# Retention and gated MLP on one core: the first pair's residual as matmuls, tiles claimed at evacuation, and a new written-out order

## The chip, the cores and the metric

The kernel runs on one core of one Trainium2 chip, with the other cores idle. The metric is device microseconds of one launch; times are medians of several runs, and a difference of about 1% is what a measurement of this kernel can tell from none. The core's engines are PE (TensorE, whose weight loads are shown apart as PEld), DVE (VectorE), ACT (ScalarE), POOL (GpSimd) and SP (SyncE, which here only issues DMAs). Each takes its own instructions in order; semaphores tie them together.

## The reference

```python
scores = scale * np.matmul(q, k.transpose(0, 1, 3, 2))
Dmat = np.where(rel >= 0, gamma[:, None, None] ** rel[None, :, :], 0.0)
ret = scores * Dmat[None, :, :, :]
x = np.matmul(ret, v)                      # 8 batches, 8 heads, 576 rows, 64 wide
...                                        # heads side by side: x is (8, 576, 512)
h = gelu(x @ w_in)                         # 512 -> 1024
u, v = h[..., :512], h[..., 512:]
v_n = (v - mu) / np.sqrt(var + 1e-06) * g_ln
v_s = np.einsum('ts,bsd->btd', w_sg, v_n) + b_sg[None, :, None]
out = x + (u * v_s) @ w_out
```

Inputs and output are float32. The output's last sum, `x +`, is the residual that the title speaks of.

## The kernel before, in words

**Tiling.** Two batches make a pair; there are 4 pairs. A pair has 2 x 576 = 1152 rows, which are 9 tiles of 128 rows; the middle tile holds the last 64 rows of both batches. The retention goes by blocks: 4 blocks of 256 rows and one block for the middle tile, 5 to a pair, 20 in all.

**Retention, per block.** q is scaled by a power of gamma, k is cast, v is scaled by the inverse power (`a_prep`, lines 391 to 405, any of ACT, DVE and POOL). q and k are transposed on PE against an identity (`a_T`, 441 for whole 128x128 tiles, 451 for 64x64 ones) and copied out of PSUM (`a_Tev`, lines 254 on ACT and 255 on DVE). PE makes the scores (`a_S`, 524), DVE multiplies them by a mask into the tile `ret` (`a_Sev`, 537 and 540). PE makes the state products k-times-v (`a_Z`, 560), whose sums over blocks DVE makes (`a_Zsum`, 585 and 588), with a bf16 copy `zb`. PE adds `ret` times v and q times state (`a_O`, 606), and ACT or DVE copy the result into `xT`, which holds x transposed (`a_Oev`, 254 and 255).

**MLP, per tile.** PE makes the v half of `x @ w_in` (`m_V`, 680), ACT its gelu into the tile `vg` (687), DVE its mean and variance (695, 696), POOL the inverse root (`m_rs`, 700 to 703), ACT or DVE the normalised `vn` (`m_norm`, 712, 714). PE makes the u half, two tiles at a time (`m_U`, 736), ACT its gelu into `uT` (747). Per batch and column group PE makes the row mixing `w_sg @ v_n` (`m_W`, 757), two PSUM tiles each, and DVE multiplies them into `uT` (767). Then, per tile, PE makes `uT @ w_out` (`m_O`, 789), and DVE adds the residual and writes the float32 tile `ob` (`m_Oev`, 806), which a DMA stores (818, or 815 twice for a middle tile).

**The residual before.** x stands transposed in `xT`. A DMA transpose on SP's queue (`m_X`, 798) brings each tile back as `xr`, and DVE adds it. The constant `XP` is the number of leading pairs that go another way: for those, four matmuls against an identity per tile add x inside PSUM (lines 782 to 787), and ACT copies the sum out (804). Before, `XP` is 0.

**What sets the order.** All work is a list of some 900 jobs. The table `ORDER` gives their order by number; a letter behind a number names the engine where several can do it (D for DVE, A for ACT, G for POOL, F for a transpose of whole tiles), and `fN` puts N filler matmuls of 128 columns on constants (`warm`) ahead of the next PSUM tile that is taken. The costs and due times written at the jobs have no effect once the table is given; only the order, the letters and the buffers count.

**Buffers.** PSUM has two pools: `pp`, 2 tiles, for transposes, scores and `a_O`; and `d`, 4 tiles, for everything else. SBUF tiles are taken in turn: `ob` 4, `xr` 5, `vg` 3, `ld` (float32 loads) 8, `ldq` 2.

**Start.** SP loads q, k, v of the first two blocks, then the next q (1 MB), the v half of `w_in` (1 MB, into `xT`'s space), further k and v, then the u half of `w_in` (1 MB, into `uT`'s space). PE's first instruction waits for three small DMAs into `rsrc` (824); DVE then works on the columns (`col_math`, 832 to 840), which give the correction rows `row4b` (851).

## Time and profile before

| what | value |
| --- | --- |
| median of 3 runs | 209.96 us (208.62 to 210.59) |
| the profiled execution's own time | 209.28 us |
| its span, first to last instruction | 207.6 us |
| around the span | 1.68 us |
| DVE, ACT, POOL busy | 79%, 56%, 54% of the span |
| queue q1 (all of SP's DMAs) | 49.28 MB, 95.5% of 16 engines' span |
| DMA transposes of `xT` into `xr` | 36, median 3.9 us from issue to landing |
| stores of 128 x 512 | 31, median 3.6 us to landing |

The profile gives busy time by engine, the chain of work that ended last, groups of instructions by line, and a timeline. A line of the timeline reads: start, duration, engine, line, operation, tile written and tiles read, shape, count, and in brackets how long the engine sat idle before it and who ended that. In the chain, "issue" is time in which the engine waited for nothing that the profile shows. The span is what the engines did; the time of a run is that plus the 1.68 us around it.

### The profile page before, as it was taken

The page shows a single profiled execution, that of the slowest core. Times are in us where ns is not written, and L with a number is a line of the kernel's source. Part 1 is how long each engine was busy: PE and PEld are TensorE (multiplying, and loading weights), DVE is VectorE, ACT ScalarE, POOL GpSimd, SP SyncE. Part 2 cuts the span into 40 slices and gives each one's busy share as a digit, 9 for nine tenths or more (in the row PEclk, how much of TensorE's full clock was granted, in tenths as well). Part 3 has the DMA queues.
Part 4 walks back from the last instruction along what each step waited for, and adds up shares of the span by engine and source line. Part 5 has one row for each costly group of instructions (what it writes and reads, how often), then busy time and mean ns, then how long its engine had stood idle before and what let it go on. Part 6 is the DMA issues. An engine that isn't in the chain of part 4 may idle for free.

```text
span 207.6 us, 7418 instructions
## 1 busy us (share of the span) xinstructions
PE 184.6 (89%) x3132; PEld 128.5 (62%) x3163; DVE 163.5 (79%) x313; ACT 115.6 (56%) x184; POOL 112.2 (54%) x163
## 2 busy tenths in 40 slices
PE   0684979989999999999999999997999999999980
PEld 0563646668777676666767866665577666575740
DVE  3879979569989887797989975999776985866661
ACT  5326677799948648797845654450838328233000
POOL 8687566978953356674959399375462220202000
PEclk9999999999999999999999999999999999999998
DMA  5999999999999999999999999899998946372656
GB/s 173 346 384 342 289 219 279 356 335 380 228 228 194 296 280 225 232 323 342 188 314 220 221 281 192 227 256 238 191 225 178 139 126 202 75 226 80 183 176 202
DMA packets 91029, 49.77 MB, mean 240 GB/s; under 512 B 42027, under 2 KB 84339, under 8 KB 90995
## 3 DMA queue, kind: packets, MB, share of 16 engines
q1 hardware_dynamic: 90976, 49.28, 95.5%
q8 instruction: 25, 0.41, 0.9%
q14 instruction: 10, 0.07, 0.1%
q10 hardware_dynamic: 18, 0.00, 0.0%
HBM read 32.94 MB, written 9.44 MB: 204 GB/s over the span
## 4 chain that ended last, share of the span: by engine, by line
PE 78%; issue 2%; DMA 2%; DVE 1%; ACT 0%; DVEq 0%; SPq 0%
PE wp L757 19%; PE hu L736 15%; PE hv L680 14%; PE op L789 13%; PE pp L606 7%; PE pp L524 3%; PE pp L441 3%; PE zp L560 2%; DMA xr<-xT 2%; PE pp L451 1%; PE wtp L878 1%; DVE ob L806 1%; ACT vg L687 0%; DVE xT L255 0%; DVE run L588 0%
## 5 line engine op out<-in xcount | busy, mean ns | idle before, releaser
L537 DVE TENSOR_TENSOR ret<-pp,msk 128x1024 bf16<-128x1024 f32 x32 | 38.4, 1213 | 3.1 <-PE pp L524 1.6
L405 POOL TENSOR_TENSOR vb<-ld,gpow 128x1024 bf16<-128x1024 f32 (+1 forms) x19 | 33.4, 1767 | 13.3 <-DMA ld<-in_v_dram 8.2
L757 PE MATMUL wp<-wT,vn 128*128 128x288 bf16 x256 | 36.8, 286 | 1.3 <-DVE run L588 1.3
L736 PE MATMUL hu<-xT,w_in 128*128 128x256 bf16 (+1 forms) x320 | 36.6, 262 | 0.5 <-DVE w_in L255 0.5
L680 PE MATMUL hv<-w_in,xT 128*128 128x512 bf16 x126 | 34.4, 379 | 2.7 <-ACT xT L254 1.4
L789 PE MATMUL op<-w_out,uT 128*128 128x512 bf16 (+1 forms) x135 | 34.2, 373 | 0.7
L767 DVE TENSOR_TENSOR uT<-wp,uT 128x288 bf16<-128x288 f32 x64 | 26.5, 448 | 9.6 <-PE wp L757 9.3
L736 PEld LDWEIGHTS <-w_in 128*128 128x128 bf16 x320 | 28.0, 98 | 7.7 <-DVE w_in L255 0.7
L687 ACT ACTIVATE vg<-hv 128x512 f32<-128x512 f32 x36 | 21.4, 595 | 18.2 <-PE hv L680 15.5
L254 ACT ACTIVATE xT<-pp 128x512 bf16<-128x512 f32 (+1 forms) x34 | 17.1, 551 | 24.0 <-PE pp L606 20.6
L700 POOL TENSOR_SCALAR mv<-mv 128x2 f32<-128x2 f32 (+1 forms) x20 | 5.1, 255 | 46.1 <-DVE mv L696 45.7
L806 DVE TENSOR_TENSOR ob<-op,xr 128x512 f32<-128x512 f32 (+1 forms) x37 | 24.5, 672 | 7.0 <-PE op L789 4.4
L757 PEld LDWEIGHTS <-vn 128*128 128x128 bf16 x256 | 24.2, 98 | 9.3 <-issue 1.5
L695 DVE BATCH_NORM_STATS2 bst<-vg 128x6 f32<-128x512 f32 x36 | 24.6, 684 | 5.3 <-ACT vg L687 5.3
L405 POOL TENSOR_TENSOR qb<-ldq,gpow 128x1024 bf16<-128x1024 f32 x13 | 25.6, 1980 | 0.7 <-DMA ldq<-in_q_dram 0.7
L712 ACT ACTIVATE vn<-vg,mv 128x512 bf16<-128x512 f32 x27 | 21.6, 810 | 7.1 <-POOL mv L703 7.0
L747 ACT ACTIVATE uT<-hu 128x512 bf16<-128x512 f32 x36 | 20.7, 594 | 7.8 <-PE hu L736 7.5
L680 PEld LDWEIGHTS <-xT 128*128 128x128 bf16 x144 | 13.5, 98 | 13.8 <-ACT xT L254 1.8
L789 PEld LDWEIGHTS <-uT 128*128 128x128 bf16 x148 | 13.7, 98 | 13.3
L701 POOL TENSOR_TENSOR mv<-mv,mhalf 128x2 f32<-128x2 f32 (+1 forms) x20 | 13.8, 690 | 1.7
L254 ACT ACTIVATE qT<-pp 128x2048 bf16<-128x2048 bf16 (+1 forms) x6 | 10.4, 1734 | 7.5 <-PE pp L441 7.5
L757 PE MATMUL wp<-wT,vmid 128*128 128x288 bf16 x64 | 13.1, 286 | 0.0
(113 smaller groups left out, 250.4 us busy)
## 6 DMA issues: line engine op xcount, KB each, us to landing
ld<-in_k_dram SPq DMA_DIRECT2D x16, 512.0 KB, 5.5
ld<-in_v_dram SPq DMA_DIRECT2D x16, 512.0 KB, 6.0
out_dram<-ob SPq DMA_DIRECT2D x31, 256.0 KB, 3.6
ldq<-in_q_dram SPq DMA_DIRECT2D x7, 1024.0 KB, 7.2
out_dram<-ob SPq DMA_DIRECT2D x10, 128.0 KB, 2.4
xT<-in_moe_w_sg_dram SPq DMA_DIRECT2D x2, 576.0 KB, 7.0
ld<-in_q_dram SPq DMA_DIRECT2D x2, 512.0 KB, 4.8
xT<-in_moe_w_in_dram SPq DMA_DIRECT2D x1, 1024.0 KB
```

The costliest lines, as they stand in the source:

```text
L254: return nc.scalar.activation(dst, src, Act.Copy)
L405: ve.tensor_tensor(dst, src, g.unsqueeze(len(src.shape) - 1).to_broadcast(list(src.shape)), op=Alu.mult)
L537: ins = nc.vector.tensor_tensor(ret[:].rearrange("p r (k t) -> p (r k) t", k=2), sc[:].rearrange("p r (k t) -> p (r k) t", k=2), (msk2 if ...
L680: ins = nc.tensor.matmul(hv[:], xTs[p][:, m, kk, :], w_in[:, kk, F2:], start=(kk == 0), stop=(kk == KK - 1))
L687: unfence(nc.scalar.activation(vgs[i][:], cur.pop(("hv", i))[:], Act.Gelu_apprx_tanh), ("V", i))
L695: nc.vector.bn_stats(bst[:], vgs[i][:])
L712: nc.scalar.activation(dst, vg[r, :], Act.Identity, scale=mv[r, s, 2:3], bias=mv[r, s, 3:4])
L736: ins = nc.tensor.matmul(hu[:, n, :], w_in[:, kk, 128 * c:128 * c + 128], xTs[p][:, m:m + w, kk, :], start=(kk == 0), stop=(kk == KK - 1), ...
L757: ins = nc.tensor.matmul(ps[half][:], vns[NT * p + tile_of(e, j)][e][:, 128 * c:128 * c + 128], wT[e][j][:, lo:lo + HS], start=(j == 0), s ...
L767: ins = nc.vector.tensor_tensor(uTs[p][:, c, col:col + HS], cur.pop(("wp", b, c, half))[:], uTs[p][:, c, col:col + HS], op=Alu.mult)
L789: ins = nc.tensor.matmul(op[:], uTs[p][:, c, r], w_out[:, c, cs], start=(p >= XP and c == 0), stop=(c == KK - 1), skip_group_check=True)
L806: ins = nc.vector.tensor_tensor(ob[:, cs], op[:], cur["xr", i][:].rearrange("p j r -> p (j r)")[:, cs], op=Alu.add)
```

## The change

`XP` becomes 1: the nine tiles of the first pair get x by four matmuls each against the identity, and ACT writes their `ob`; nine DMA transposes go. The tiles `ret`, `vg` and `ob` are taken by the job that writes them and no longer by the matmul ahead of it. `vg` has 4 tiles (3), `mv` 4 (3), `vn` 13 (11). The stores of the last pair may go on ACT's queue. The scaling of v of the first block and of q of the second are put behind the column arithmetic in the planner's dependencies. `ORDER` is new, with more fillers: `f15 f24` ahead of PE's first instruction, `f11` later.

```diff
-    XP = 0
+    XP = 1
...
-BUFS = dict(... vg=3, mv=3, vn=11, ob=4, xr=5, pp=2, d=4)
+BUFS = dict(... vg=4, mv=4, vn=13, ob=4, xr=5, pp=2, d=4)
...
     def a_S(b, g):
-        st[b, "ret", g] = new("ret", [128, 2, 512], BF)
     def a_Sev(b, g):
-        ret = st[b, "ret", g]
+        ret = st[b, "ret", g] = new("ret", [128, 2, 512], BF)
...
     def m_V(i):
-        vgs[i] = new("vg", [128, F2], F32)
     def m_Vg(i):
+        vgs[i] = new("vg", [128, F2], F32)
...
     def m_O(i, hf=None):
-        if not hf:
-            cur["ob", i] = new("ob", [128, DM], F32)
     def m_Oev(i, hf=None):
+        if ("ob", i) not in cur:
+            cur["ob", i] = new("ob", [128, DM], F32)
...
-    def m_store(i, hf=None):
+    def m_store(i, hf=None, eng="SP"):
+        dma = nc.sync if eng == "SP" else nc.scalar
...
-                               deps=[J["ld", b, "q"]] + jqs, ...
+                               deps=[J["ld", b, "q"]] + ([j_cm] if b == 1 else []), behind=jqs[0] if c else None, ...
-        jvv = add("POOL", ..., deps=[J["ld", b, "v"]], ...
+        jvv = add("POOL", ..., deps=[J["ld", b, "v"]] + ([j_cm] if not b else []), ...
...
-    "2 3 8 4 97 9 75 98D 0 100F 10 1 78 14 102D 101A 81 79 ...
+    "2 f15 3 4 f24 8 97 9 75 98 0 10 1 100F 78 14 74 99 101 5 ...
```

In the program this removes 16 of the 64-wide transposes and adds 8 of 128 (all counted as matmuls), adds 36 residual matmuls with their weight loads and 9 filler instructions, moves 9 `ob` from DVE to ACT, and moves copies of transposed tiles from ACT to DVE (ACT loses four of 128x2048 into `qT` and one into `kT`; DVE gains the same). POOL gives five scalings of v and q to DVE and takes one. On SP the nine transposes of the first pair go and six store instructions move to ACT. In the first loads, v of the first block goes ahead of q of the second, and the u half of `w_in` goes ahead of v of the third block.

**Place 1: PE, end of the first pair's middle block.** The last state products of the retention are followed by the v half's products before:

```order
L606 LDWEIGHTS zb
L606 MATMUL pp<-qT,zb 64x128
L606 LDWEIGHTS zb
L606 MATMUL pp<-qT,zb 64x128
L680 LDWEIGHTS xT
L680 MATMUL hv<-w_in,xT 128x512
L680 LDWEIGHTS xT
L680 MATMUL hv<-w_in,xT 128x512
```

and now by eight products of the u half:

```order
L605 LDWEIGHTS zb
L605 MATMUL pp<-qT,zb 64x128
L605 LDWEIGHTS zb
L605 MATMUL pp<-qT,zb 64x128
L735 LDWEIGHTS w_in
L735 MATMUL hu<-xT,w_in 128x256
L735 LDWEIGHTS w_in
L735 MATMUL hu<-xT,w_in 128x256
```

The v half's products of the tiles that these blocks write come later by a group of eight.

**Place 2: DVE, ahead of the third pair's first row mixing.** `run` is the sum of state products, read out of two `d` tiles. Before, a `vn` stands between the two reads:

```order
L806 TENSOR_TENSOR ob<-op,xr 128x512
L537 TENSOR_TENSOR ret<-pp,msk_81 128x1024 x2
L806 TENSOR_TENSOR ob<-op,xr 128x512 x2
L585 COPY run<-zp 128x256
L714 TENSOR_SCALAR vn<-vg,mv 128x512
L588 TENSOR_TENSOR run<-zp,run 128x256
L806 TENSOR_TENSOR ob<-op,xr 128x512
```

and now a `ret`:

```order
L584 COPY run<-zp 128x256
L536 TENSOR_TENSOR ret<-pp,msk_81 128x1024
L587 TENSOR_TENSOR run<-zp,run 128x256
L536 TENSOR_TENSOR ret<-pp,msk_81 128x1024
L805 TENSOR_TENSOR ob<-op,xr 128x512
L766 TENSOR_TENSOR uT<-wp,uT 128x288 x2
```

On PE, the group of row mixing that follows the state products came after 16 score and 4 output matmuls; it now comes after 32 score, 16 u half and 4 output matmuls.

**Place 3: SP, the end.** Before, the last transpose stands behind two stores, and six more store instructions behind it (with tile numbers, since the rows read alike):

```order
L798 DMA_TRANSPOSE xr_4725<-xT_3748 128x4x128
L818 DMA out_0_dram<-ob_4728 128x512
L818 DMA out_0_dram<-ob_4736 128x512
L798 DMA_TRANSPOSE xr_4759<-xT_3748 128x4x128
L818 DMA out_0_dram<-ob_4751 128x512
L815 DMA out_0_dram<-ob_4743 64x512 x2
L818 DMA out_0_dram<-ob_4762 128x512
L818 DMA out_0_dram<-ob_4771 128x256 x2
```

Now SP ends so:

```order
L795 DMA_TRANSPOSE xr_4681<-xT_3784 128x4x128
L795 DMA_TRANSPOSE xr_4699<-xT_3784 128x4x128
L795 DMA_TRANSPOSE xr_4715<-xT_3784 128x4x128
L818 DMA out_0_dram<-ob_4672 128x512
L818 DMA out_0_dram<-ob_4697 128x512
L795 DMA_TRANSPOSE xr_4767<-xT_3784 128x4x128
L818 DMA out_0_dram<-ob_4794 128x512
L818 DMA out_0_dram<-ob_4802 128x256 x2
```

and ACT, which has no other work by then, so:

```order
L746 ACTIVATE uT_3837<-hu_4663 128x2x256
L818 DMA out_0_dram<-ob_4674 128x512
L818 DMA out_0_dram<-ob_4759 128x512
L815 DMA out_0_dram<-ob_4769 64x512 x2
L818 DMA out_0_dram<-ob_4778 128x512
L818 DMA out_0_dram<-ob_4785 128x512
```

The two stores that the last transpose stands behind are now those of tiles written before the last eight row mixings; four of the five last full tiles are stored from ACT, and three store instructions are left behind the transpose.

## The prediction

> **What bounds the kernel now.** I read the page's first two parts, then the stretches of the span one by one, then the chain of waits, and last the timeline where a stretch has a hole. The first rows are the page's:

> ```profile
> span 207.6 us, 7418 instructions
> PE 184.6 (89%) x3132; PEld 128.5 (62%) x3163; DVE 163.5 (79%) x313; ACT 115.6 (56%) x184; POOL 112.2 (54%) x163
> PE 78%; issue 2%; DMA 2%; DVE 1%; ACT 0%; DVEq 0%; SPq 0%
> ```

> PE is busy for 89% of the span and holds 78% of the chain that ended last. By stretches (busy us of PE, PEld, DVE, ACT, POOL):

> ```profile
> 0.00:31.00 31.00, 18.65 (x400) 13.88 (x403) 24.32 (x55) 16.55 (x21) 22.82 (x41) 1.00 0.97 293
> 31.00:197.00 166.00, 161.37 (x2708) 112.42 (x2737) 134.79 (x252) 99.09 (x164) 89.33 (x123) 1.00 0.99 233
> 140.00:150.00 10.00, 8.64 (x148) 5.55 (x147) 8.59 (x15) 4.23 (x9) 5.66 (x5) 1.00 0.94 221
> 197.00:207.60 10.60, 4.61 (x26) 2.25 (x24) 4.37 (x8) 0.00 (x0) 0.00 (x0) 0.93 0.64 192
> ```

> From 31 to 197 us PE is idle for only 4.6 of 166 us, and 1.4 of these lie between 140 and 150. The time to be had is in three places: 12.3 us idle in the first 31, the hole at 140, and 6.0 us of tail after PE's last matmul, which ends at 201.6. Anything that adds PE work between 31 and 201 costs its full length, because nothing covers it.

> **Term 1, the residual by matmuls: +2.0 us.** 36 matmuls of 128 columns, each with its own weight load, stand ahead of output groups. The nearest rows of the chain are transposes, which have the same shape (128x128 weights, 128 columns), and a weight load's own length:

> ```profile
> 64.00 0.89 PE pp L441 x16
> 66.12 0.86 PE op L789 x4
> L789 PEld LDWEIGHTS <-uT 128*128 128x128 bf16 x148 | 13.7, 98 | 13.3
> 60.39 0.57 PE pp L451 x32
> ```

> 0.89/16 = 56 ns a pair, so 36 x 56 = 2.0 us. Bounds: 0 if all fell into holes, which 161.37 of 166 excludes for nearly all; 36 x 98 ns = 3.5 us if each weight load showed. I take 2.0, since the transposes load new weights for each matmul too. [...]

> The transposes' changed form adds 8 x 56 - 16 x 18 ns (0.57/32) = +0.2 us. Nine `ob` of 0.69 us leave DVE and cost ACT about 0.6 each (an ACT copy of 128x512 into `xT` has 595 ns), 5.4 us. In this stretch ACT also loses work: before, it makes one `qT` and three `kT` of 1.88 us and two `kb` of 1.06 between 60 and 100 us, which is 9.6; in the new order one `kT`, one half `qT` and one `kb`, which is 4.0.

> ```profile
> 60.00:100.00 40.00, 39.55 (x785) 27.26 (x791) 33.96 (x60) 30.11 (x45) 20.55 (x30) 1.00 1.16 259
> L254 ACT ACTIVATE kT<-pp 128x2048 bf16<-128x2048 bf16 x3 | 5.6, 1877 | 1.5 <-PE pp L441 1.4
> L391 ACT ACTIVATE kb<-ld 128x1024 bf16<-128x1024 f32 x3 | 3.2, 1056 | 0.0
> L254 ACT ACTIVATE xT<-pp 128x512 bf16<-128x512 f32 x27 | 15.1, 595 | 20.9 <-PE pp L606 18.3 <-DVE xT L255 2.6
> ```

> So ACT stays near 30 of 40 us, and I cost the move at 0; its cover is the other `d` tiles that PE has, and without it every output group would hold PE for up to a copy's 0.6 us, 5.4 in all. The nine transposes that go free SP and the DMA engines (1.16 busy share), but PE waits for neither there: 0.

> **Term 2, the start: -0.9 us.** The first score matmul hangs on this chain:

> ```profile
> 6.17 0.69 DVE L393 CAST qb<-ld 128x1024 bf16<-128x1024 f32 x1 [0.21 <-DMA ld<-in_k_dram]
> 6.92 1.89 PE L441 MATMUL pp<-ident,qb 128*128 128x128 bf16 x16 [1.11 <-DVE qb L393]
> 8.85 1.88 ACT L254 ACTIVATE qT<-pp 128x2048 bf16<-128x2048 bf16 x1 [3.55 <-PE pp L441]
> 10.78 0.64 PE L524 MATMUL pp<-qT 64*64 64x128 bf16 x16 [0.92 <-ACT qT L254]
> ```

> Now k is cast on ACT (1.06 us, the mean of the `kb` casts there), ending at 7.2. The 16 transposes take 1.89 here against 0.89 later: PE starts slow, although the granted clock reads 1.00. Fillers ahead of it, 39 x 128 columns, cost 39 x (1.89/16) = 4.6 us at the slow pace; if they start at 1.0, they end at 5.6, just when `rsrc` is there (PE's first matmul starts at 5.57 now). So they cost nothing and the transposes end at about 8.2. DVE has finished the column arithmetic (8.66 now, 0.7 earlier without the cast) and copies `qT` in 1.21: the first scores come at 9.5, a lead of 1.2 us. If the fillers don't help, it is 0.2.

> That lead then meets the loads:

> ```profile
> 20.49 1.40 POOL L393 CAST kb<-ld 128x1024 bf16<-128x1024 f32 x1 [1.11 <-DMA ld<-in_k_dram]
> 23.50 1.90 POOL L405 TENSOR_TENSOR vb<-ld,gpow 128x1024 bf16<-128x1024 f32 x1 [1.61 <-DMA ld<-in_v_dram]
> 28.08 0.69 DVE L255 CAST w_in<-uT 128x1024 bf16<-128x1024 f32 x1 [0.78 <-DMA uT<-in_moe_w_in_dram]
> 38.45 0.68 DVE L540 TENSOR_TENSOR ret<-pp,msk 128x512 bf16<-128x512 f32 x1
> ```

> The k and the v between 20.49 and 23.50 take 1.5 us each (512 KB), `w_in`'s half 4.6 (1 MB, 23.50 to 28.08). With `w_in` ahead of v it lands at 22.0 plus 3.0 (by bytes) to 4.6 (its own row); I take 4.3, nearer its own row, 26.3, and for v 27.8, so the third block's v is scaled at 29.7, where it was at 25.4. DVE starts at 26.3 on a run without a gap: the cast 0.69, four statistics of 0.86, four `ret` of 1.21, four sums of 0.41, and a q, a `vn`, a `qT` and a small `ret` of 0.6 to 0.7, together 13.2. The small `ret` ends at 39.5, where it ended at 39.1 before, and PE's products behind it start at 39.5 against 40.2, with one u half group of 0.87 less done: 0.2 us behind. So the loads and DVE's run eat the whole lead.

> Then comes place 1, with these rows of the chain:

> ```profile
> 41.47 0.43 DVE xT L255
> 41.93 0.39 ACT xT L254
> 42.32 0.28 issue
> 42.60 0.81 PE hv L680 x3
> ```

> PE stood for 1.1 us until `xT` was copied; now eight u half matmuls of 0.87 us stand in that gap. So 1.1 less 0.2 is the gain of the start: 0.9. Bounds: 0 if DVE's run comes out one microsecond longer, 2.3 (1.2 + 1.1) if `w_in` lands at k's and v's pace and the first lead survives.

> **Term 3, the hole at 140: -1.9, and +0.9 for new ones.**

> ```profile
> 139.06 0.42 DVE L585 COPY run<-zp 128x256 f32<-128x256 f32 x1 [0.40 <-PE zp L560]
> 139.41 1.84 DVE L714 TENSOR_SCALAR vn<-vg,mv 128x512 bf16<-128x512 f32 x1
> 141.16 0.41 DVE L588 TENSOR_TENSOR run<-zp,run 128x256 f32<-128x256 f32 x1
> 141.63 1.02 PE L757 MATMUL wp<-wT,vn 128*128 128x288 bf16 x7 [1.30 <-DVE run L588]
> ```

> The row mixing needs a `d` tile that the second `run` frees, and a `vn` of 1.84 us stands ahead of that. At place 2 the two reads now have a `ret` of 1.21 between them, 2.0 in all, while PE has 0.57 of scores, 1.74 of u half and 0.86 of output to do: the hole (139.68 to 141.59) closes. But an order that is new from end to end makes holes of its own. The order before has 4.6 us of them from 31 to 197, of which this one and place 1 are 3.0; half of such a hole, 0.9, is my value for what the new one adds, with 0 and 3.8 (two whole ones) as ends.

> **Term 4, the tail: -1.0.** The end hangs on SP's queue; first two pieces of the chain, then rows of the timeline:

> ```profile
> 198.91 0.33 SPq L818
> 199.29 3.57 DMA xr<-xT
> ```
> ```profile
> 196.26 5.35 PE L789 MATMUL op<-w_out,uT 128*128 128x512 bf16 x27
> 199.29 2.06 SPq L798 DMA_TRANSPOSE xr<-xT  x1
> 201.45 0.53 SPq L818 DMA_DIRECT2D out_dram<-ob  x1
> 201.87 0.69 DVE L806 TENSOR_TENSOR ob<-op,xr 128x512 f32<-128x512 f32 x1 [1.26 <-DMA out_dram<-ob]
> 202.98 0.76 DVE L806 TENSOR_TENSOR ob<-op,xr 128x256 f32<-128x256 f32 x2 [0.42 <-DMA xr<-xT]
> 203.27 1.52 SPq L818 DMA_DIRECT2D out_dram<-ob  x3
> ```

> The last transpose waits behind a store of a tile finished at 198.9, lands at 202.9, and holds DVE's two half tiles; the stores wait behind it and behind each other, until 204.8. At place 3 the stores ahead of it are of tiles done before the last row mixings, 6 us earlier, so it is in time. What is late next is `ob`: four tiles, so the fifth of the last six waits for the store of the first (1.26 us now), issued at 198.05 and 3.6 us long, until about 201.7; the halves wait for the store of the second, until 202.5. They end at 203.3 and the last issue at 203.8, against 204.8: -1.0. Bounds: 0, if the `ob` tiles come back no sooner, and -1.6, the transpose's hold on the halves (0.4) and the queue's on the stores (1.2) both gone.

> The larger `vg`, `mv` and `vn`, the claims at evacuation and the moves between DVE and ACT cost 0: they free PE of nothing that it waits for in the rows. What hides them is DVE's 20% of idle time.

> **The sum.** 207.6 + 2.0 + 0.2 - 0.9 - 1.9 + 0.9 - 1.0 = 206.9 of span; with the 1.68 around it 208.6 us, against 209.28 of the same execution, 0.3% less. The median of the runs shown is 209.96, which is 0.7 us above that execution. About 1% is what a measurement of this kernel can tell from no change.

> **Rivals.**

> *All holes close.* The start keeps 2.3, the tail 1.6, and no hole comes back: 207.6 + 2.2 - 2.3 - 1.9 - 1.6 = 204.0, 205.7 us. For it: each hole has its own named cause in the rows, and the new order treats each. Against: `w_in` took 4.6 us, not 3.0.

> *The row mixing waits for state sums.* In the new order the row mixing of the second and third pair follows state products at three places with only four products (0.2 us) between. If the mixing there needs a tile that DVE's second `run` frees, each place costs what the one at 140 did, 1.9: three for the 0.9 that I allow give 208.6 - 0.9 + 5.7 = 213.4 us, slower by 2.0%. It decides once DVE makes the second `run` over 1 us behind the product. For it: DVE has a `bn` or a copy between the two reads at each. Against: the tiles ahead of the state products in the ring of four are free by then.

> *The start gives nothing.* The loads pace it, place 1 waits for DVE instead: 208.6 + 0.9 = 209.5, no difference. *Weight loads show*: a matmul of 128 columns waits for part of its 98 ns load, halfway between 56 and 98, so 36 x 77 ns: 209.4, no difference. [...]

> **How the numbers follow.** My forecast has a chance of 0.42, with its own range 207.0 to 210.2; all holes close 0.33; the row mixing waits 0.15; the start gives nothing 0.06; weight loads show 0.04. A time under 207.9 is faster by over 1%: the second case, and 0.07 of the first, 0.40 together. Over 212.1 is slower: the third case, 0.15. The rest is 0.45. The range reaches into both outer cases, 205.0 to 212.5.

> **What would show it.** Right: 36 residual matmuls with about 56 ns each in the chain; PE's last matmul ends near 201.5; no PE wait near the third pair's first row mixing; the first scores near 9.5 us; `w_in`'s u half cast near 26.3; no `xr` in the chain's end, and 5 us from PE's last matmul to the end. Wrong: PE idle for over 6 us between 31 and 197, above all ahead of row mixings with "DVE run" as the releaser; ACT over 36 of 40 us busy in the first pair's outputs; or a start whose 31 us hold less PE work than 18.65.

## The result, and the profile after

The changed kernel takes **216.53 us** (median of 4, 216.18 to 216.58) where the kernel before took 209.76 in the same session (208.62 to 210.59): a ratio of 1.032, 95% interval 1.027 to 1.037. It is slower by 3.2%, and the forecast of 208.6 with its range to 212.5 was wrong. The profiled execution took 216.56 us, its span 214.9, which is 8.0 more than the 206.9 of the sum. (Of the kernel shifted by 208 places, below, one execution of 383.5 us ran every matmul from 12 us on at half pace; it is left out of what follows.)

First the page of the changed kernel: the span, the engines, and the chain that ended last, by engine.

```profile
span 214.9 us, 7475 instructions
PE 193.3 (90%) x3173; PEld 132.5 (62%) x3200; DVE 160.5 (75%) x301; ACT 116.7 (54%) x196; POOL 109.0 (51%) x163
PE 76%; DMA 6%; issue 5%; SPq 4%; ACT 4%; DVE 3%; POOL 1%; ACTq 0%; DVEq 0%; POOLq 0%
```

"issue" is up from 2% to 5% of the chain. Then the same kernel by stretches (span, its length, then busy us of PE, PEld, DVE, ACT and POOL, the granted clock, DMA share and GB/s):

```profile
31.00:204.00 173.00, 163.99 (x2689) 113.80 (x2712) 132.19 (x239) 98.34 (x169) 87.70 (x126) 0.98 0.82 213
40.00:45.00 5.00, 4.57 (x48) 2.31 (x38) 2.24 (x6) 3.18 (x7) 2.26 (x5) 0.66 1.05 313
60.00:100.00 40.00, 37.80 (x681) 26.20 (x684) 31.78 (x52) 27.34 (x47) 17.20 (x25) 1.00 0.74 221
140.00:204.00 64.00, 63.17 (x877) 42.69 (x885) 49.07 (x96) 28.11 (x49) 20.03 (x37) 1.00 0.75 178
```

PE is idle for 9.0 of 173 us, where before it was idle for 4.6 of 166. After 140 little is lost (63.17 of 64.00), so the hole at 140 did close and the loss lies ahead of it. PE's timeline shows where: three stops in the middle of a group of equal matmuls, none of which a semaphore ends.

```profile
37.55 0.39 PE L605 MATMUL pp<-ret,vb 64*64 64x128 bf16 x14
39.79 0.47 PE L605 MATMUL pp<-ret,vb 64*64 64x128 bf16 x18 [1.86 <-issue]
...
61.04 0.49 PE L451 MATMUL pp<-ident,qb 64*128 64x64 bf16 x21
63.41 0.33 PE L451 MATMUL pp<-ident,qb 64*128 64x64 bf16 x11 [1.88 <-issue]
...
103.73 0.46 PE L559 MATMUL zp<-vb,kb 64*64 64x64 bf16 x26
106.95 0.26 PE L559 MATMUL zp<-vb,kb 64*64 64x64 bf16 x1 [2.76 <-issue]
```

PE stops after 14 of 32 matmuls, after 21 of 32, after 31 of 32 (five of these 31 stand between scores, ahead of the line shown). These read the same tiles as their neighbours and write the same PSUM tile, so a wait for another engine's work is unlikely there, and the profile names none. Together they are 6.50 us.

**Numbering PE's stream.** In the built program each matmul is two instructions of PE (weight load and product), and there are a few waits. Laid against the trace by line and count, the matmuls at which PE resumes have the places 1218, 1985 and 3522 in a stream of 6421. These are 4 x 256 + 194, 7 x 256 + 193 and 13 x 256 + 194. The page's list of DMA queues (packets, MB, share) has a queue with a period of its own:

```profile
q1 hardware_dynamic: 85344, 46.79, 80.9%
q8 instruction: 25, 0.41, 0.8%
```

25 packets of 0.41 MB are 16 KB each, 6421 places in 25 pieces are 257 each, and the three places lie 3 x 256 - 1 and 6 x 256 + 1 apart. From these numbers I estimate that PE's stream arrives in packets of 256 instructions, which makes 64 bytes for one; the page counts the packets' time on the 16 DMA engines that carry the loads (0.8% beside 80.9%). The kernel shifted by 208 places, below, has 6629 places and 26 packets. The prediction had not weighed this queue.

**When a packet comes.** The DMA queues, by tenths of a microsecond, give the time at which each packet is on the engines. There are 25 packets and 25 boundaries, one for each: in the changed kernel the packet with the next piece of the stream appears as late as 4.1 to 4.7 us after PE has entered the current one (seen at 133.1, PE's entry between 128.4 and 129.0).

| kernel | PE enters the piece | packet seen from | PE at its end | PE resumes | stall | resumes after packet |
| --- | --- | --- | --- | --- | --- | --- |
| changed | 33.57 | 37.5 | 37.93 | 39.79 | 1.86 | 2.3 |
| changed | 58.14 | 61.0 | 61.53 | 63.41 | 1.88 | 2.4 |
| changed | 100.56 | 104.4 | 104.19 | 106.95 | 2.76 | 2.5 |
| before, its fastest piece | 57.29 | 58.4 | 61.61 | 61.63 | none | |

These are the three pieces that PE of the changed kernel uses up fastest: 4.4, 3.4 and 3.6 us, made of output products, state products, scores and small transposes in a row, where 256 places elsewhere last 5.2 to 17. The fastest of the kernel before takes 4.3 us, and its packet came 1.1 us after the entry.

**Theory A**: PE stops where it has used up its 256 instructions before the next packet has come, because the new order puts short matmuls in a row while the DMA engines are full (a share of 1.12, 1.07 and 1.14 from the three entries to the packets; it is 1.24 in the piece of the kernel before, whose packet came 1.1 us after the entry). **Rival B**: the stops are waits of those places in the program. **Rival D**: the fillers and the start cost the time.

**The pace behind a stop.** Behind the first and third stop PE runs slowly for a few us. The same groups of the changed kernel, and of the kernel shifted by 160 places below, which has no stop there:

```profile
42.47 2.95 PE L678 MATMUL hv<-w_in,xT 128*128 128x512 bf16 x7 [0.22 <-ACT xT L254]
```
```profile
41.08 1.67 PE L690 MATMUL hv<-w_in,xT 128*128 128x512 bf16 x7
```

From the u half behind the products to the next transposes it is 5.17 us (40.96 to 46.13) against 3.48 (39.98 to 43.46), and from the row mixing to the next transposes 6.40 (107.31 to 113.71) against 5.15 (100.83 to 105.98): 1.69 and 1.25 lost, 2.9 together. The granted clock (the last figure but two of a line by stretches) is down in these two places, and not behind the second stop, which is as long as the first:

```profile
41.70:45.00 3.30, 3.08 (x9) 1.24 (x9) 0.57 (x3) 2.13 (x5) 1.37 (x4) 0.50 0.96 308
63.50:70.00 6.50, 6.45 (x119) 4.67 (x120) 4.82 (x10) 4.29 (x5) 0.00 (x0) 1.00 0.84 242
106.60:109.80 3.20, 2.85 (x16) 1.80 (x17) 1.55 (x4) 1.65 (x3) 2.43 (x2) 0.50 1.06 202
```

A clock of 0.66 over 40 to 45 (and over 105 to 110) is 3.4 us at 0.50 (5 x 0.34/0.50), which by that figure can cost 1.7 us of work. The stops and the slow pace are 6.5 + 2.9 = 9.4 us: without both the span would be 205.5.

### The profile page after: what moved, and what is told of

It is laid out like the page before. It is cut to its first block, busy times and chain, and to the rows that moved or that the text cites. A ratio compares the mean times of both kernels' runs of the same rounds, so it can differ in the third digit from the quotient of the medians.

```text
span 214.9 us, 7475 instructions
## 1 busy us (share of the span) xinstructions
PE 193.3 (90%) x3173; PEld 132.5 (62%) x3200; DVE 160.5 (75%) x301; ACT 116.7 (54%) x196; POOL 109.0 (51%) x163
## 3 DMA queue, kind: packets, MB, share of 16 engines
q1 hardware_dynamic: 85344, 46.79, 80.9%
## 4 chain that ended last, share of the span: by engine, by line
PE 76%; DMA 6%; issue 5%; SPq 4%; ACT 4%; DVE 3%; POOL 1%; ACTq 0%; DVEq 0%; POOLq 0%
PE wp L756 19%; PE hv L678 14%; PE hu L735 13%; PE op L786 13%; PE pp L605 6%; DMA xT<-in_moe_w_in_dram 4%; PE pp L523 4%; SPq L351 4%; PE pp L441 3%; PE zp L559 2%; ACT xT L254 1%; DMA out_dram<-ob 1%; PE op L781 1%; DVE ret L536 1%; ACT w_in L254 1%
## 5 line engine op out<-in xcount | busy, mean ns | idle before, releaser
L756 PE MATMUL wp<-wT,vn 128*128 128x288 bf16 x256 | 37.8, 291 | 0.0
L678 PE MATMUL hv<-w_in,xT 128*128 128x512 bf16 x129 | 36.0, 392 | 1.5 <-ACT xT L254 0.5
L735 PE MATMUL hu<-xT,w_in 128*128 128x256 bf16 (+1 forms) x320 | 37.1, 263 | 0.0
L405 POOL TENSOR_TENSOR vb<-ld,gpow 128x1024 bf16<-128x1024 f32 (+1 forms) x16 | 27.9, 1742 | 14.1 <-DMA ld<-in_v_dram 12.0
L254 ACT ACTIVATE xT<-pp 128x512 bf16<-128x512 f32 (+1 forms) x37 | 18.8, 555 | 24.9 <-PE pp L605 19.7
L699 POOL TENSOR_SCALAR mv<-mv 128x2 f32<-128x2 f32 (+1 forms) x20 | 6.1, 305 | 49.8 <-DVE mv L695 49.4
L746 ACT ACTIVATE uT<-hu 128x512 bf16<-128x512 f32 x36 | 20.9, 593 | 17.2 <-PE hu L735 17.1
L805 DVE TENSOR_TENSOR ob<-op,xr 128x512 f32<-128x512 f32 (+1 forms) x28 | 18.5, 669 | 9.5 <-PE op L786 7.2
L405 POOL TENSOR_TENSOR qb<-ldq,gpow 128x1024 bf16<-128x1024 f32 x11 | 21.6, 1971 | 5.5 <-issue 5.5
L711 ACT ACTIVATE vn<-vg,mv 128x512 bf16<-128x512 f32 x28 | 22.2, 806 | 2.7 <-POOL mv L702 2.6
L678 PEld LDWEIGHTS <-xT 128*128 128x128 bf16 x144 | 13.8, 101 | 15.1 <-issue 2.2
L605 PE MATMUL pp<-ret,vb 64*64 64x128 bf16 (+1 forms) x576 | 12.4, 214 | 1.9 <-issue 1.9
L756 PE MATMUL wp<-wT,vmid 128*128 128x288 bf16 x64 | 13.3, 291 | 0.0
```

The source lines that it names most:

```text
L254: return nc.scalar.activation(dst, src, Act.Copy)
L405: ve.tensor_tensor(dst, src, g.unsqueeze(len(src.shape) - 1).to_broadcast(list(src.shape)), op=Alu.mult)
L605: nc.tensor.matmul(ot[64 * c:64 * c + 64, bank, j * cs:(j + 1) * cs], lhsT, rhs, start=(bank, c) not in begun, stop=True, skip_group_check ...
L678: ins = nc.tensor.matmul(hv[:], xTs[p][:, m, kk, :], w_in[:, kk, F2:], start=(kk == 0), stop=(kk == KK - 1))
L711: nc.scalar.activation(dst, vg[r, :], Act.Identity, scale=mv[r, s, 2:3], bias=mv[r, s, 3:4])
L735: ins = nc.tensor.matmul(hu[:, n, :], w_in[:, kk, 128 * c:128 * c + 128], xTs[p][:, m:m + w, kk, :], start=(kk == 0), stop=(kk == KK - 1), ...
```

## Experiments: moving the stream

Three kernels get small matmuls in PE's idle time at the start, which do nothing but push every later instruction on; in the two made from the changed kernel they stand in place of its six widest fillers. The code, in the helper that takes a PSUM tile:

```diff
+        for x in range(cur.pop("small", 0)):
+            c = slice(64 * (x % 2), 64 * (x % 2) + 64)
+            nc.tensor.matmul((t if dtype == F32 else t[:].bitcast(F32))[c, :64], warm[:64, :64], warm[:64, :64], start=True, stop=True, skip_group_check=True)
```

**Changed kernel, 208 places.**

```diff
-    "2 f15 3 4 f24 8 97 ...
+    "2 f15 3 4 s110 8 97 ...
```

> The changed kernel with its six widest fillers replaced by 110 small matmuls (64x64, in the idle time before the first transposes), so that every later TensorE instruction stands 208 places further on in TensorE's own stream. Nothing else is changed. Theory A (the three stalls of 1.86, 1.88 and 2.76 us come where TensorE crosses into the next 256 instructions of its stream before these have arrived over the instruction queue): the stalls at the second column block's output matmuls, the transposes L451 and the state matmuls are gone, no issue stall over 1 us is left or one at most, the granted clock between 35 and 110 us reads 1.00, and the time is 207 to 210 us. Rival B (the stalls are waits that belong to those places of the program, a buffer or an evacuation): they stay at the same matmuls with the same lengths and the time stays at 216 to 217 us.

Ratio 1.026 (1.016 to 1.036); three executions took 213.0, 216.1 and 217.2 us. That is neither theory's number. It ran a second time:

> The kernel of the 208 places a second time, for a profile that can be read: in the first one every matmul from 12 us to the end ran at half its speed (383.5 us), and the other three runs took 213.0 to 217.2 where theory A gave 207 to 210. From the runs so far the 256 instructions after index 194 modulo 256 can be run about 2.7 us after their packet starts on the DMA engines, and a packet waits 0 to 4 us for its turn. Theory A in this form: whatever the time is over that of the 160 places (208.2) is made of stalls of TensorE marked issue, each at an index of 193 to 195 modulo 256 and each about 2.7 us less the time between the packet and TensorE's arrival, with granted clocks under 1.00 behind some of them. Theory E (the small matmuls at the start themselves cost the time, over the start or the clock): no such stall, and the loss lies in the first 20 us or in a low clock all along.

212.0 us in the profiled execution, 216.1 in the other. The PE timeline has two stops, and no other of over 0.3 us by issue:

```profile
41.24 0.64 PE L617 MATMUL pp<-qT,zb 64*64 64x64 bf16 x11 [1.03 <-issue]
...
65.52 0.77 PE L453 MATMUL pp<-ident,kb 128*128 128x128 bf16 x11 [1.78 <-issue]
```

They are at places 1471 and 2241, which is 191 and 193 modulo 256 (a few matmul records are missing, so that the count is good to some places). Their packets were seen from 38.8 and 63.1, 2.4 us ahead of the resumption, where I had put about 2.7. So the shift did move the stops to other instructions, against B. My forecast for it failed because I had gone by the length of the pieces alone (5.0 us and more): one packet came 4.7 us after PE had entered its piece.

**Changed kernel, 160 places.**

```diff
-    "2 f15 3 4 f24 8 97 ...
+    "2 f15 3 4 s86 8 97 ...
```

> The same with 86 small matmuls, a shift of 160 places. By the times at which the changed kernel's matmuls ran, the 256-instruction pieces are then used up slowest everywhere except one that begins near 114 us and lasts 3.3 us. Theory A: the three old stalls are gone, at most one stall of 1 to 2.5 us near 115 us in their place, where the index is again 194 modulo 256; 207 to 212 us. Rival B: three stalls where they were, 216 to 217 us.

**208.19 us** (median of 10, 207.33 to 209.0) against 208.87; ratio 0.9975 (0.9937 to 1.0013). Page, and PE by stretches:

```profile
span 207.3 us, 7635 instructions
PE 190.8 (92%) x3253; PEld 133.0 (64%) x3280; DVE 160.1 (77%) x301; ACT 116.6 (56%) x196; POOL 108.4 (52%) x163
```
```profile
31.00:197.00 166.00, 162.60 (x2750) 114.00 (x2768) 133.22 (x242) 98.61 (x170) 89.02 (x128) 1.00 0.85 226
```

No stop by issue of over 0.3 us is left; each packet was on the engines at least 2.4 us before PE needed it, the clock reads 1.00, and PE is idle for 3.4 of 166 us. The same work in the same order, but for fillers, is 3.4% or 7 us faster at other places of the stream (0.9975 against 1.0323 of the kernel before). That the places do it and not the fillers taken out is seen from the kernel of 208 places: it lacks the same six and has stops. The stall that I thought possible at 115 did not come.

**Kernel before, 96 places.**

```diff
-    "2 3 8 4 97 ...
+    "2 s48 3 8 4 97 ...
```

> The kernel before with 48 small matmuls in the idle time ahead of its first transposes, a shift of 96 places and nothing else. The piece of its stream that begins near 97 us is then used up in 3.2 us. Theory A: one stall of 1 to 3 us inside a group of matmuls near 100 us that the kernel before does not have, at an index of 194 modulo 256, and 210 to 213 us; the hole of 1.3 us at 140 us, which is not at such an index, stays. Rival B: 209 to 210.5 us, no new stall.

```profile
101.59 0.26 PE L536 MATMUL pp<-qT,kT 64*64 64x128 bf16 x4
102.77 0.36 PE L536 MATMUL pp<-qT,kT 64*64 64x128 bf16 x12 [0.91 <-issue]
...
144.43 1.02 PE L769 MATMUL wp<-wT,vn 128*128 128x288 bf16 x7 [1.39 <-DVE run L600]
```

The stop came where it was forecast, at place 3522, 194 modulo 256, 2.3 us after its packet was seen (100.5). It is 0.9 us and not 1 to 3, and the time does not show it (ratio 0.9986, 0.9948 to 1.0023); the execution with the profile was the longest of the ten, 211.24 us. The hole at 140 us stays, at a place that is no boundary: that one is DVE's, as the prediction had it.

**Changed kernel without fillers.**

```diff
-    "2 f15 3 4 f24 8 ... 272 288 f11 273 ...
+    "2 3 4 8 ... 272 288 273 ...
```

> The changed kernel without its 13 filler matmuls, which also moves the stream 26 places ahead (shortest pieces 4.6 us near 58 us and 4.8 us near 34 us, where they were 3.4, 3.6 and 4.4). Theory A: the stalls are shorter by the second or so that the pieces gain, or gone: 208 to 214 us. Rival D (the fillers at the start cost the time, since the granted clock reads 0.75 and 0.57 from 5 to 15 us): first scores at 10.4 us or before, a clock of 1.00 from 5 to 15 us, and at most 2 us gained in the first 20 us with the three stalls as they were, 214.5 to 216.5 us.

214.34 us, ratio 1.022 (1.015 to 1.030).

```profile
39.64 0.30 PE L605 MATMUL pp<-ret,vb 64*64 64x128 bf16 x5 [1.31 <-issue]
63.66 1.46 PE L678 MATMUL hv<-w_in,xT 128*128 128x512 bf16 x6 [1.98 <-issue]
105.74 0.42 PE L756 MATMUL wp<-wT,vmid 128*128 128x288 bf16 x2 [0.81 <-issue]
```

With 13 matmuls fewer the stops are at the places 1218, 1985 and 3522 again, but 26 instructions further on in the program: behind 27 of 32 products and no longer 14, within the v half behind the transposes, within the row mixing. This is the clearest single sign against B: the place in the stream stays, the instruction changes. They resume 2.4, 2.6 and 2.3 us after their packets were seen (37.3, 61.1, 103.4). Two are shorter, one is not; 4.1 us in all. D falls too: the first scores come at 10.60, 0.24 later than with fillers.

## Experiments: what the packets wait for

The stalled packets had loads of 1 MB (`ldq`) issued ahead of them (at 28.93 and 37.20, at 55.29, and at 98.83 in the changed kernel). Two of these loads move to a later place in SP's order, with PE's stream as it was:

```diff
-    27 48 372 ... 217 51 138 ...          398 61 504 ...          407 59 573 ...
+    27 372 ... 217 51 48 138 ...          398 504 ...             407 59 61 573 ...
```

> The changed kernel, its stream not shifted, with two of SyncE's loads of 1 MB issued later: the q load that stands at 55.3 us moves behind the two loads after it (to about 61), and the q load at 98.8 behind the next v, store and k (to about 104). The loads ahead of the first stall stay as they are. Theory A with its cause in the DMA queues (a packet of instructions waits for the bytes issued ahead of it: 1 MB and 1 MB before the one asked for at 58.1, 1 MB before the one at 100.6): the first stall stays at 1.9 us, the second and the third shrink from 1.88 and 2.76 to under 1 each or vanish, 211 to 214 us unless a q then comes late. Rival (the wait of a packet does not depend on what was issued ahead): all three stay, 216 to 217 us.

212.25 us, ratio 1.014 (1.009 to 1.020). PE's timeline, then SP's:

```profile
40.31 0.47 PE L605 MATMUL pp<-ret,vb 64*64 64x128 bf16 x18 [2.11 <-issue]
...
63.77 0.33 PE L451 MATMUL pp<-ident,qb 64*128 64x64 bf16 x11 [1.73 <-issue]
...
104.93 0.21 PE L559 MATMUL zp<-vb,kb 64*64 64x64 bf16 x1 [0.36 <-issue]
...
112.77 0.46 PE L605 MATMUL pp<-ret,vb 64*64 64x128 bf16 x17 [1.10 <-issue]
```
```profile
58.16 2.87 SPq L351 DMA_DIRECT2D ldq<-in_q_dram  x1
...
102.91 0.95 SPq L351 DMA_DIRECT2D ldq<-in_q_dram  x1
```

The first stop, whose loads were not touched, stays. The third shrinks from 2.76 to 0.36: its packet is seen 1.7 us after PE enters the piece (100.86, 102.6) where it was 3.9. A new stop comes at place 3778, one packet later, for which the moved load now stands ahead (packet seen 110.4, PE had entered the piece at 104.93). The second stays; that load had gone out at 58.16, still ahead of PE's entry into the piece at 58.61. When a packet is asked for, no run shows: some appear before PE enters the piece ahead of theirs, so the entry is at most a guide. So both loads were moved past those points:

```diff
-    27 48 372 ... 388 49 439 ...          398 61 504 ...          530 511 ...
+    27 372 ... 388 49 48 439 ...          398 504 ...             530 61 511 ...
```

> The changed kernel, not shifted, with the same two q loads of 1 MB moved further, so that each is issued after TensorE has entered the piece whose successor came late: the one of 55.3 us to about 62 (entry at 58.6; before it, at 58.16, it was still ahead and the second stall stayed at 1.73), the one of 98.8 to about 107 (entries at 100.9 and 104.9; at 102.9 it stood ahead of the second of them and a stall of 1.10 came there). Theory A with its cause in the DMA queues: the first stall stays at 1.9 to 2.1 us, none is left at 61 to 64, 104 to 107 and 112 us, 209 to 211.5 us. Rival (only the third place hangs on the loads): the stall at 63 stays at 1.7, 211 to 213 us.

211.74 us, ratio 1.010 (1.002 to 1.018).

```profile
39.10 0.47 PE L605 MATMUL pp<-ret,vb 64*64 64x128 bf16 x18 [0.90 <-issue]
...
61.27 0.33 PE L451 MATMUL pp<-ident,qb 64*128 64x64 bf16 x11 [1.67 <-issue]
...
118.96 0.62 PE L441 MATMUL pp<-ident,qb 128*128 128x128 bf16 x8 [2.72 <-POOL qb L393]
```

The stops at 104 to 107 and at 112 are gone, so these hang on that load. The first is 0.90, where it was 1.86 and 2.11 with nothing ahead of it changed: a stop's length varies by about a microsecond between executions, less than the 2.4 by which the third shrank. The second is not cured although `ldq` now leaves at 58.20, 2 us after PE has entered the piece at 56.16; the packet is still seen 2.6 us after that entry. My cause for that one falls, and what its packet waited for stays open (the 1 MB of `w_out` left at 52.43, and k and v behind it). Part of the gain is given back at 119, where the late q holds the transposes for 2.72.

## Experiments: the terms of the sum

**The residual by matmuls alone**, in the old order: the constant, and the nine transposes as jobs that do nothing.

```diff
-    XP = 0
+    XP = 1
-                    if p >= XP:
-                        jX = add("SP", 1000.0, due - 6000.0, lambda i=i: m_X(i), ...
+                    jX = add("SP", 1000.0, due - 6000.0, (lambda i=i: m_X(i)) if p >= XP else (lambda: None), ...
```

> The kernel before with one part of the change alone: the first pair's residual by 36 matmuls, its output tiles copied by ACT, and its nine transposes gone; order, buffers and all else as before. Term 1 of the prediction: 2.0 us more than the kernel before, with pairs of about 56 ns, and 0 for the copies that move to ACT. Rivals: each weight load shows, 3.5 us more; ACT's copies come late for the output groups, up to 5.4 more; the transposes had slowed the DMA engines, so that less than 1 is left of the 2.0. Behind the first pair's outputs TensorE's stream stands up to 72 places further on, so a stall at 194 modulo 256 is possible and is to be taken off by its length.

210.72 us; ratio 1.0072 (1.0035 to 1.011), so 1.5 us more (0.7 to 2.3). The chain of the changed kernel has the pairs, the timeline of this one the only wait of PE for ACT's copies:

```profile
90.48 0.33 PE op L781 x4
...
97.41 0.22 PE op L781 x4
```
```profile
103.64 0.44 PE L560 MATMUL zp<-vb,kb 64*64 64x64 bf16 x31 [0.40 <-ACT ob L804]
```

0.22/4 is 55 ns a pair. Six of the nine groups have 0.22 in the chain and three 0.33, 2.3 us in all. There is no stop by issue of over 0.3 us, and the copies hold PE once for 0.40.

**A filler in the gap ahead of the first transposes**, on the kernel of the 160 places (8 places more, for the four new fillers).

```diff
-    ... 10 1 100F 78 ...
+    ... 10 1 f16 100F 78 ...
```

> The kernel of the 160 places with four more fillers of 512 columns between the transposition of the norm's row (5.7 us) and the first transposes (7.3 us), where TensorE stood idle. Term 2 of the prediction had the fillers make those 16 transposes fast. If it is the idle gap of 1.6 us that spoiled it, the 16 now take 0.9 to 1.2 us and not 1.7 to 1.9, the first scores come at 9.5 to 9.9 instead of 10.5, and the time falls by 0 to 0.9. Rival: TensorE's pace at the start does not hang on work just before; the 16 take 1.7 to 1.9 as they did, first scores at 10.5, no gain.

```profile
2.76 2.50 PE L239 MATMUL tp<-warm 64*64 64x64 bf16 x86
...
5.51 1.89 PE L235 MATMUL pp<-warm 128*128 128x512 bf16 x4
7.32 1.68 PE L453 MATMUL pp<-ident,qb 128*128 128x128 bf16 x16
10.31 0.42 PE L535 MATMUL pp<-qT 64*64 64x128 bf16 x16 [1.32 <-DVE qT L267]
```

PE has worked since 1.04 without a gap of note, and the 16 transposes still take 1.68; only the scores behind them are at their later pace (0.42, not 0.64). Ratio 0.9971 (0.9935 to 1.0007), the same as without. But 2.5 of these 6.3 us are small matmuls of 64x64, and only the last 1.9 are wide fillers again, so this run does not settle what the wide ones do.

The changed kernel's own start does. Of its ten wide fillers, from 1.04 us on, seven take 2.96 us (0.42 each) and the last three 0.80 (0.27 each): PE's pace goes up at about 4.0, behind 3.0 us of work. But the fillers end at 4.8, PE then does 0.2 us of work until the transposes at 7.29, and during these the pace falls again. Here are the stretches of 7.3 to 9.1 us, first of the changed kernel, then of the two with moved loads (in the order above), whose start is the same:

```profile
7.30:9.10 1.80, 1.74 (x16) 1.47 (x16) 0.74 (x6) 0.00 (x0) 1.38 (x2) 0.55 1.15 346
```
```profile
7.30:9.10 1.80, 1.16 (x16) 0.89 (x16) 1.32 (x6) 0.00 (x0) 1.38 (x2) 0.72 1.15 347
7.30:9.10 1.80, 1.06 (x16) 0.88 (x16) 1.23 (x5) 0.00 (x0) 1.26 (x1) 0.82 1.15 346
```

The granted clock falls to 0.50 at about 7.5, 8.1 and 8.5 us, and the 16 transposes take 1.74, 1.18 and 1.07. (In the kernels where the pace did not rise ahead of the transposes these take 1.68 to 1.89. In the kernel before, with 1.89, the clock reads 1.00 from 6.90 to 8.82 all the same, so that reading does not tell the pace.)

**The same kernel with small fillers only.**

```diff
-    "2 f15 3 4 s86 8 ... 272 288 f11 273 ...
+    "2 s93 3 4 8 ... 272 288 273 ...
```

> The kernel of the 160 places without any of the 13 wide fillers: 93 small matmuls at the start give the same shift. Term 2 of the prediction had the wide fillers give 1.0 us at the start. From the kernel without fillers (first scores at 10.60 against 10.36) they give 0.2 at most: 207.8 to 208.6 us beside 208.2 to 208.9 for the kernel of the 160 places, no issue stall. Rival (the fillers matter after all): first scores 1 us later or a slower pace after them, 209.2 or more.

209.34 us, ratio 1.0001 (0.9967 to 1.0036). The time is more than I forecast and within the rival's 209.2 or more, but the kernel before took 209.26 beside it, and the rival's signs are not there: the first scores come at 10.50, as with the wide ones, and there is no stop by issue of over 0.3 us. The intervals of this kernel and of the one with fillers overlap, so a gain of the fillers is not shown.

**The last stores back on SP's queue**, also on the kernel of the 160 places.

```diff
-    ... 839A ... 843A ... 886A ... 875A ... 871A ...
+    ... 839 ... 843 ... 886 ... 875 ... 871 ...
```

> The kernel of the 160 places with the five stores of the last pair that ACT issues back on SyncE's queue. Term 4 of the prediction gave the tail 1.0 us, of which the last transposes' place in the queue is one part and the stores' own queue the other. If the gain is the queue's, the end from TensorE's last matmul is 0.5 to 1.2 us longer than in the kernel of the 160 places, and the time 208.7 to 209.4; if it is the transposes' place alone, there is no difference (208.0 to 208.4).

Ratio 0.9982 (0.9944 to 1.002): no difference. The end from PE's last matmul is 5.4 us (200.48 to 205.9), and 5.2 with ACT's queue (202.12 to 207.3). By these two executions the queue is worth 0.2.

## Why the prediction was wrong, by its own steps

**Where it failed.** Term 3 allowed 0.9 us for new holes, "half of such a hole", with two whole ones, 3.8, as the far end. They came to 6.5, with 2.9 of slow pace behind them: 8.5 more than allowed, where the span missed the sum by 8.0. The allowance was worked out from waits that the profile of before names: buffers, evacuations, tiles. None of its rivals holds a wait for PE's own instructions. The step that shut it out is in term 1: the freed DMA time counts 0, since "PE waits for neither there". PE does wait for the DMA engines, through queue q8 (the third stop went from 2.76 us to 0.36 when a load of 1 MB was moved), and the page of before listed that queue as the page of after does, with 25 packets and 0.41 MB. What could have been worked out ahead is how many us PE spends on each 256 places, in the new order against the old: the fastest piece of the old order takes 4.3 us, three of the new one 4.4, 3.4 and 3.6. That the packet comes 2.8 to 3.9 us behind the entry in these three, only the new trace shows.

**What held.** With the stops moved out of the way, the ratio is 0.9975 (0.9937 to 1.0013), and the sum had said 0.3% less. That agreement is in part luck: two terms were too large as gains, one as a cost.

- *Term 1*, +2.0 (and 0.2): 2.3 us in the chain, +1.5 us (0.7 to 2.3) alone. Right, within what these can tell. ACT was 27 of 40 us busy from 60 to 100, forecast near 30, never over 36.
- *Term 2*, -0.9: its first step failed. The first scores came at 10.36 and not 9.5, since the 16 transposes took 1.74 us and not 1.0. The fillers did raise PE's pace, but they ended at 4.8 and not at 5.6, and the pace fell again among the transposes; in the two kernels with moved loads it fell later, and the scores came at 9.78 and 9.68. The lead was worth nothing even so: eight transposes further on wait for POOL's `qb` in all three and start at 33.27 in both of these, at 33.00 in the changed kernel. That the loads eat the lead was forecast. Place 1 was counted from the chain as 1.1 us, but PE's idle time there was 0.75 (first line below). The u half of `w_in` was there earlier than I had it (its casts start at 24.2 and 24.95, forecast 26.3). Taking the other terms off the profiled span of the kernel of 160 places (207.3 = 207.6 + 1.7 for term 1 and the transposes' form, less 1.2 us of idle PE between 31 and 197, less 0.8 of tail), nothing is left for the start. That is one execution against one, so it is good to about a microsecond.
- *Term 3*, -1.9: the hole at 140 is closed. That DVE caused it is borne out by the kernel before shifted by 96 places, where it stays. But it was worth 1.3: the prediction's own line has PE idle for 1.30 ahead of 141.63, and the 1.9 from 139.68 on took in matmuls that still ran. With 1.30 and 0.75 closed out of 4.6, and 3.4 left in the kernel of 160 places, the new order's own holes come to 0.9, as allowed, where no packet is late.
- *Term 4*, -1.0: right (the first line is the kernel before at place 1, for term 2; the others are the changed kernel's tail).

```profile
42.60 0.81 PE L680 MATMUL hv<-w_in,xT 128*128 128x512 bf16 x3 [0.75 <-ACT xT L254]
```
```profile
204.55 5.35 PE L786 MATMUL op<-w_out,uT 128*128 128x512 bf16 x27
206.33 1.22 SPq L795 DMA_TRANSPOSE xr<-xT  x1
209.78 2.27 SPq L818 DMA_DIRECT2D out_dram<-ob  x3
210.49 0.76 DVE L805 TENSOR_TENSOR ob<-op,xr 128x256 f32<-128x256 f32 x2 [0.74 <-DMA out_dram<-ob]
```

In the tail PE's last matmul ends at 209.90, the span at 214.9, 5.0 us as forecast; `xr` is in time, and what holds the halves is an `ob` tile, as the term had it. ACT's queue has about 0.2 of it.

**The rivals.** The row mixing that waits for state sums did not happen: no row mixing of the later pairs waits for a `run`. Its sign was met for another reason, PE idle for over 6 us between 31 and 197. The start did give nothing, but that rival's 209.5 leaves out the stops. Weight loads did not show: 2.3 us for 36 pairs is 64 ns each. A version that clearly beats the kernel before has not come out of this: the four kernels of 160 places (one of 168) lie at 0.9971, 0.9975, 0.9982 and 1.0001.

**What stays open**: what the second stop's packet waits for, when a packet is asked for, and why the granted clock falls to 0.50 behind four of the fifteen stops (1.31 to 2.76 us long) and not behind the others (0.36 to 1.98).

## What to carry to other kernels

A stop of PE in the middle of a group of equal matmuls, marked issue, is to be looked up by its place in PE's stream: if such places differ by multiples of 256, as 1218, 1985 and 3522 did here within one place, PE may have run out of instructions. Before an order is judged, look at how many us each 256 instructions take and what loads are queued when PE enters the piece; a run of short matmuls, each with its own weight load, beside full DMA queues is where it broke here (3.4 to 4.4 us for 256 places, a DMA share of 1.07 to 1.14). Then the number of instructions ahead is a knob of its own, and two orders are compared at more than one shift before a few per cent are put down to the work.
